# Three rotating tiles for transposed probabilities, later low halves and a later comparison step in a fused attention and expert kernel

## The chip, the core and the metric

The kernel runs on one core of a Trainium2 chip. The metric is the device time of one execution in microseconds, taken as the median of several runs; lower is better. The engines are named as the profile names them: PE is TensorE (PEld its weight loads), DVE is VectorE, ACT is ScalarE, POOL is GpSimd, SP is SyncE, which here only issues DMAs.

## What is computed

Attention over 4 batches, 8 heads, 576 positions and 64 dimensions, with a mask that keeps only scores near the row's maximum; then a feed-forward layer with a rational activation, then a second layer of experts. Cut to what matters:

```python
scores = scale * np.matmul(q, k.transpose(0, 1, 3, 2))
thresh = np.max(scores, axis=-1, keepdims=True) - tau
scores = np.where(scores >= thresh, scores, -1000000000.0)
attn = np.exp(scores - np.max(scores, axis=-1, keepdims=True))
attn = attn / (np.sum(attn, axis=-1, keepdims=True) + 1e-09)
x = np.matmul(attn, v)                      # then tokens x 512
h = x @ w_in                                # w_in, w_out arrive as float64
g = (a[0] + a[1]*h + a[2]*h**2 + a[3]*h**3) / (1.0 + abs(b[0])*abs(h) + abs(b[1])*h**2 + 1e-6)
x = g @ w_out                               # then top-1 routing over 8 experts
y[mask] = gate_w[mask, None] * (np.maximum(xc[mask] @ w1[e], 0.0) @ w2[e])
```

## The kernel before

**Precision.** Products that need more than one pass are made from a rounded high half and a low half (the value less its rounding). For K and Q, `high` (L256, L257) scales and rounds on ACT, and `low` (L268) subtracts on POOL. The weights `w_in` and `w_out` arrive as pairs of 32-bit words; `decode` turns them into single precision on DVE, POOL and ACT and then into two halves. It is a generator: each call runs on to the next `yield`, and `PACE_A` says how many calls lie between its steps. The steps are: load, shift (L115), merge (L117), `lf` on POOL (L121) with the exponent mask on DVE (L124), a product (L126), Abs on ACT (L129) and a sum on POOL (L130), the comparison and product on DVE (L133; on POOL, L135 and L136, for every fourth chunk), rounding on POOL (L142) and the low half (L146). The tile `w`, written by L129 and last read by L146, has one buffer, as have `t1` and `lf`.

**Tiling of attention.** Two heads make a pair, 16 pairs in all. Each pair has nine half tiles of queries (slots (r, h), r from 0 to 4), and the loop takes two slots a turn, so that a pair lasts 4.5 turns and there are 72 turns. In a turn, by the string `SEQ`, stand for the slots: the row minimum of the (negated) scores (M, L284), the threshold (H, L296), the exponential (E, L292), the products with V (V, L356 and L360), two evacuations of transposed tiles from the turn before (X, Y, L334), the output copy xT (W, L371), two entries of the task list (K, K), decoding (D, twice a turn), the mask with its sum (A, L302), the scores of the next turn's slots (N, L278), and the transposes of this turn's (t, L314). Each engine runs its own part of this string in order and waits on semaphores for the others. The order is thus written by hand.

**Buffers.** Scores have two PSUM buffers, so the scores of a slot of the next turn wait for the mask of this turn's. `P` holds the masked exponentials of an r (both h); four buffers, and two of `PL` for r = 4. The transposes of one pair go to `PT(p,0)` (r = 0, 1; 256 columns) and `PT(p,1)` (r = 2, 3, 4; 320 columns), one buffer each. At the end of a group one more tile T_x collects the last columns: for (p,1) it reads P(p,2) and P(p,3) (L321) and `PL` (L323, L324). The product with V of a group is ten steps (eight L356 matmuls in four pairs, two L360 with the remainder VZ), accumulated in the single PSUM buffer O. Its steps are handed out by a credit: each turn adds `CR`, up to `CAP` = 1.4, each step takes 0.48 or 0.59, and the turns with a T_x pay a surcharge. xT goes to DRAM (L375, L376) once a pair, after the second group.

**Tasks.** When a pair's first slot comes up, the loads of the pair after next are issued and eight tasks are listed for the next pair: high and low of two pieces of K and two of Q in turn. Two are taken each turn.

After turn 70 the pools of the stage close and the feed-forward units follow (`ffn1`, `actA` and on), then the experts.

Of the kernel before, what the change touches and what calls it, by code (L numbers as in the profile page):

```python
# [9 lines left out]
F32 = mybir.dt.float32  # L10
# [25 lines left out]
RG = (6, 8, 8)  # L36
C897 = 1.125 * 2.0 ** -15
DB = {"raw": 2, "t1": 1, "lf": 1, "w": 1}
PACE_A = (8, 1, 1, 1, 1, 2, 2, 2, 3)
PACE_B = (2, 1, 1, 1, 0, 1, 1, 0, 4)  # L40
CR = 1.4


@with_exitstack
def body(ctx, tc, q, k, v, tau, w_in, w_out, a, b, w_skip, w_gate, w1, w2, out):
# [6 lines left out]
    P = 128  # L52
# [147 lines left out]
    with ExitStack() as actx:  # L200
# [86 lines left out]
        def expo(p, r, h):  # L287
            st, m = St[p, r, h]
            if h == 0:
                Pt[p, r] = ap2.tile([P, 1152 if r < 4 else 576], F32, tag="P" if r < 4 else "PL", bufs=4 if r < 4 else 2, name=f"P{p}_{r}")  # L290
            e = Pt[p, r][:, 576 * h:576 * h + 576].rearrange("p (c x) -> p c x", c=2)
            nc.scalar.activation(e, st, AF.Exp, bias=m[:, 0:1], scale=-1.0)  # L292
            St[p, r, h] += [e]
# [12 lines left out]
        def transp(p, r, h):  # L306
            pt = Pt[p, r]
            g = 0 if r < 2 else 1
            if (p, g) not in PT:
                PT[p, g] = ap1.tile([P, 10, 256 if g == 0 else 320], F32, tag=f"PT{g}", name=f"PT{p}_{g}")  # L310
            T = psT.tile([P, 512], F32, tag="T", name=f"T{p}_{r}_{h}")
            for j in range(4):
                j0 = 128 * (5 * h + j)
                nc.tensor.transpose(T[:, 128 * j:128 * j + 128], pt[:, j0:j0 + 128], idn)  # L314
            Tt[p, r, h] = T
            if (r, h) not in ((1, 1), (4, 0)):
                return
            credit[0] -= 0.25 if r < 4 else 0.45
            T = Tt[p, r, 2] = psT.tile([P, 512], F32, tag="T", name=f"T{p}_{r}_x")
            for j in range(2):  # L320
                nc.tensor.transpose(T[:, 128 * j:128 * j + 128], Pt[p, 2 * g + j][:, 512:640], idn)  # L321
            if r == 4:
                nc.tensor.transpose(T[:, 256:384], Pt[p, 4][:, 448:576], swp)  # L323
                nc.tensor.transpose(T[0:64, 256:384], Pt[p, 4][:, 512:576], idn)  # L324
# [39 lines left out]
        def xout(p, g):  # L364
            bi, hp = divmod(p, NHP)
            o = Ot[g]
            w = 256 if g == 0 else 320
            if g == 0:
                xTs[p] = ap2.tile([P, 576], F32, tag="xT", name=f"xT{p}")
            xT = xTs[p]  # L370
            nc.scalar.activation(xT[:, 256 * g:256 * g + w], o[:, :w], AF.Copy)  # L371
            if g == 0:
                return
            c0, cl = xcols(bi)
            dq.append(lambda: [nc.sync.dma_start(xTd[:, hp, c0:c0 + 512], xT[:, 0:512]),  # L375
                               nc.sync.dma_start(xTd[:, hp, cl:cl + 64], xT[:, 512:576])])  # L376
            if hp == NHP - 1:
                wact.append(norm(bi))

        def norm(bi):  # L380
# [83 lines left out]
        for i in range(NS // 2 + 2):  # L464
# [4 lines left out]
            for x in cur:  # L469
                if x[1:] == (0, 0):  # L470
                    load(x[0] + 2)
                    n = x[0] + 1
                    for z in ((0, 0, 432), (0, 432, NK), (1, 0, 608), (1, 608, NQ)):
                        tasks += [(high, n, *z), (low, n, *z)]
                elif x[1:] == (2, 0):
                    loadv(x[0] + 1)
            mm = ap2.tile([P, 4], F32, tag="m", bufs=4, name=f"m{i}")
# [2 lines left out]
            for op in SEQ.split():  # L480
# [18 lines left out]
                elif c == "N" and j < len(nxt):  # L499
                    smm(*nxt[j])  # L500
                elif c == "M" and j < len(cur):
                    soft(*cur[j], mm[:, j:4:2])
                elif c == "H" and cur:
                    thr(mm)
                elif c == "E" and j < len(cur):
                    expo(*cur[j])
                elif c == "A" and j < len(cur):
                    mask(*cur[j])
                elif c == "T" and j < len(old):
                    transp(*old[j])  # L510
                elif c == "X" and j < len(old):
                    evac(*old[j])
                elif c == "Y" and j < len(old):
                    evac(*old[j])
                elif c == "t" and j < len(cur):
                    transp(*cur[j])
                elif c == "x" and j < len(cur):
                    evac(*cur[j])
                elif c == "V":
                    while pvq and credit[0] > 0 and not (xq and pvq[0][2] == 0):  # L520
                        credit[0] -= 0.48 if pvq[0][1] == 0 else 0.59
                        pv(*pvq.pop(0))
                elif c == "W":
                    while xq:
                        xout(*xq.pop())
                elif c == "K" and tasks:
                    fn, *n = tasks.pop(0)
                    fn(*n)
                elif c == "D" and i < 70:
                    wstep()  # L530
                elif c == "L":
                    for fn in late:
                        fn()
# [508 lines left out]
```

## Time and profile before

| what | us |
|---|---|
| median of 3 runs | 1034.93 (1033.43 to 1038.8) |
| the profiled execution | 1033.06 |
| its span, first to last instruction | 1031.2 |
| busy in the span: PE, DVE, ACT, POOL | 927.3, 698.6, 618.1, 480.2 |
| stage of attention (first row minimum to the last turn) | 13.6 to 363 |

The profile is of one execution. A row of the list of waits tells which engine and line stood idle, until what had ended, for how long in total, how often, and the longest. A row of the timeline tells the start, the duration, the engine, the line, the operation, what it writes and reads, and in brackets how long the engine had been idle and what ended that. Names are the program's, without buffer numbers.

### The profile page before, as it was taken

The numbers are of one execution on the slowest core, as the hardware profiler recorded it, in microseconds if no ns is written. First come the engines' busy times: TensorE is split into PE (matmuls) and PEld (weight loads), VectorE is DVE, ScalarE is ACT, GpSimd is POOL, SyncE is SP. The second block draws the span as 40 slices with busy tenths as digits, with TensorE's granted clock in tenths as the row PEclk, the third lists the DMA queues.
The fourth block names the chain that finished last, engine by engine and source line by source line (L and its number), as shares of the span: only waits on it lengthen the run. The fifth ranks groups of instructions, "written<-read, shape, count | busy, mean of one in ns | idle before, by whom it ended". The sixth has DMA issues, their size and how long they took to land.

```text
span 1031.2 us, 15811 instructions
## 1 busy us (share of the span) xinstructions
PE 927.3 (90%) x5442; PEld 760.5 (74%) x5442; DVE 698.6 (68%) x1450; ACT 618.1 (60%) x1153; POOL 480.2 (47%) x484
## 2 busy tenths in 40 slices
PE   3888888778768989999999999999998999999996
PEld 2556555555545668877888889889887888899885
DVE  4978877776776849989899987787776633211221
ACT  4777866767567757877777777777777611111110
POOL 1556548557557515678997663323334800000000
PEclk9989999888889999999999999999999999999998
DMA  5435345445262520434344232433424761313101
GB/s 152 110 103 154 88 135 137 137 119 162 92 185 63 186 79 23 147 103 147 113 170 156 75 123 103 140 127 106 171 92 158 251 215 62 123 61 123 62 31 33
DMA packets 72101, 124.14 MB, mean 120 GB/s; under 512 B 14928, under 2 KB 47184, under 8 KB 72016
## 3 DMA queue, kind: packets, MB, share of 16 engines
q1 hardware_dynamic: 67696, 99.48, 31.1%
q0 software_dynamic: 4320, 23.59, 6.6%
q8 instruction: 45, 0.74, 0.3%
q14 instruction: 40, 0.33, 0.1%
HBM read 85.22 MB, written 37.82 MB: 119 GB/s over the span
## 4 chain that ended last, share of the span: by engine, by line
PE 57%; POOL 11%; DVE 11%; issue 7%; ACT 7%; DMA 3%; SPq 2%; POOLq 0%; DVEq 0%; ACTq 0%
PE h L190 12%; PE acc L605 12%; PE mhs L190 10%; PE Ys L605 10%; PE S L278 4%; PE T L314 3%; PE O L356 3%; POOL Q L268 2%; POOL lf L126 1%; DVE m L284 1%; DVE p L634 1%; ACT P L292 1%; DVE h L649 1%; DVE p L646 1%; DVE h L647 1%
## 5 line engine op out<-in xcount | busy, mean ns | idle before, releaser
L605 PE MATMUL acc<-wo,g 128*128 128x512 f32 x864 | 223.4, 401 | 11.2 <-ACT g L655 8.2
L605 PEld LDWEIGHTS acc<-wo,g 128*128 128x128 f32 x864 | 158.7, 189 | 52.5 <-ACT g L655 13.0
L624 POOL TENSOR_TENSOR qd<-v,qd 128x384 f32<-128x384 f32 x96 | 98.5, 1026 | 188.0 <-ACT v L621 175.5
L278 PE MATMUL S<-K,Q 64*128 64x288 f32 x960 | 101.9, 337 | 78.4 <-DVE P L302 65.7
L190 PE MATMUL h<-xg,wi 128*128 128x384 f32 x864 | 165.2, 340 | 0.0
L278 PEld LDWEIGHTS S<-K,Q 64*128 64x128 f32 x960 | 76.9, 203 | 119.0 <-issue 83.0
L190 PEld LDWEIGHTS h<-xg,wi 128*128 128x128 f32 x864 | 152.1, 188 | 4.8 <-issue 0.4
L292 ACT ACTIVATE P<-S,m 128x576 f32<-128x576 f32 x144 | 101.0, 739 | 59.8 <-DVE m L284 59.3
L302 DVE SCALAR_TENSOR_TENSOR P<-S,m,P 128x576 f32<-128x576 f32 x144 | 111.5, 811 | 31.4 <-ACT P L292 31.3
L851 DVE SCALAR_TENSOR_TENSOR mgs<-mhs,mgs 128x384 fp32r<-128x384 f32 x48 | 26.8, 558 | 152.0 <-ACT mgs L850 152.0
L850 ACT ACTIVATE mgs<-mhs 128x384 fp32r<-128x384 f32 x48 | 23.6, 492 | 171.9 <-PE Ys L605 168.7
L284 DVE TENSOR_REDUCE m<-S 128x1 f32<-128x576 f32 x144 | 104.4, 753 | 28.6 <-PE S L278 26.6
L190 PE MATMUL mhs<-mxs,wss 128*128 128x384 f32 x576 | 109.2, 338 | 0.0
L605 PE MATMUL Ys<-wss,mgs 128*128 128x512 f32 x432 | 108.4, 396 | 0.0
L190 PEld LDWEIGHTS mhs<-mxs,wss 128*128 128x128 f32 x576 | 101.7, 188 | 4.0
L314 PE MATMUL T<-idn,P 128*128 128x128 f32 x576 | 93.7, 308 | 2.4 <-DVE P L302 2.3
L605 PEld LDWEIGHTS Ys<-wss,mgs 128*128 128x128 f32 x432 | 80.1, 188 | 16.1
L334 ACT ACTIVATE PT<-T 128x512 f32<-128x512 f32 x128 | 71.2, 600 | 28.4 <-PE O L360 28.2
L314 PEld LDWEIGHTS T<-idn,P 128*128 128x128 f32 x576 | 72.2, 157 | 16.3 <-issue 11.0
L629 DVE TENSOR_TENSOR p<-p,h 128x384 f32<-128x384 f32 x96 | 52.7, 549 | 43.9 <-ACT p L623 43.7
L356 PE MATMUL O<-PT,V 128*64 128x320 f32 (+1 forms) x512 | 79.6, 435 | 0.0
L268 POOL TENSOR_TENSOR K<-rk,K 128x432 fp32r<-128x432 f32 x30 | 33.8, 1125 | 94.1 <-ACT K L257 85.4
(149 smaller groups left out, 1547.5 us busy)
## 6 DMA issues: line engine op xcount, KB each, us to landing
xg<-xSd POOLq DMA_DIRECT2D x18, 768.0 KB, 5.7
x2Td<-x2h SPq DMA_DIRECT2D x12, 768.0 KB
mxs<-x2Td POOLq DMA_DIRECT2D x12, 768.0 KB, 5.6
rq<-in_q_dram SPq DMA_DIRECT2D x30, 304.0 KB, 4.3
raw<-in_moe_w_in_dram SPq DMA_DIRECT2D x16, 512.0 KB, 4.5
raw<-in_moe_w_out_dram SPq DMA_DIRECT2D x16, 512.0 KB, 3.9
rk<-in_k_dram SPq DMA_DIRECT2D x80, 72.0 KB, 3.0
xSd<-px SPq DMA_DIRECT2D x24, 192.0 KB, 1.9
```

The costliest lines, as they stand in the source:

```text
L190: nc.tensor.matmul(h, w[:, sw, 128 * k:128 * k + 128], x[:, sx, k], start=(k == 0 and i == 0), stop=(k == NKT - 1 and i == 2))
L268: eng.tensor_tensor(t[:, 1], x, t[:, 0].bitcast(F32), op=ALU.subtract)
L278: nc.tensor.matmul(st[:, c, :288], Q[d, x, q0:q0 + P], K[d, y, k0:k0 + 288], start=(s == 0 and j in (0, h)), stop=(s == 2 and (r < 4 or j ...
L284: nc.vector.tensor_reduce(m[:, 0:1], st, axis=AX.XY, op=ALU.min)
L292: nc.scalar.activation(e, st, AF.Exp, bias=m[:, 0:1], scale=-1.0)
L302: nc.vector.scalar_tensor_tensor(e, st, m[:, 1:2], e, op0=ALU.is_le, op1=ALU.mult, accum_out=sums[:, bi, col, hp:hp + 1])
L314: nc.tensor.transpose(T[:, 128 * j:128 * j + 128], pt[:, j0:j0 + 128], idn)
L334: nc.scalar.activation(dst[:, 5 * h:5 * h + 4, c0:c0 + 128], T.rearrange("p (j c) -> p j c", c=128), AF.Copy)
L356: nc.tensor.matmul(o[d, :w], vts[p][:, x, j, :], pt[:, j + 5 * x, :], start=(j == 0), stop=False)
L605: nc.tensor.matmul(ac[t], g[:, sg, 128 * t:128 * t + 128], w[:, sw, :], start=(first and i == 0), stop=(last and i == 2))
L624: nc.gpsimd.tensor_tensor(qd, v, u, op=ALU.mult)
L629: nc.vector.tensor_tensor(p, p, hs[c, f], op=ALU.mult)
```

## The change

PT becomes one tag with three buffers of the larger size for both groups. P goes from four buffers to three and PL from two to one. xT is split in two tiles of one buffer each, one for each group, and each is stored as soon as its group is done: three DMAs a pair where there were two. `CR` goes from 1.4 to 1.45. The task list is written in eight entries in which a low half stands one turn behind its high half, except the last; the rounding tasks keep their turns. In `PACE_A` the comparison step L133 (or L135 and L136) comes one call later, the rounding L142 too, and the low half L146 at the same call as before.

```diff
--- before.py
+++ after.py
@@ -36,9 +36,9 @@
 RG = (6, 8, 8)
 C897 = 1.125 * 2.0 ** -15
 DB = {"raw": 2, "t1": 1, "lf": 1, "w": 1}
-PACE_A = (8, 1, 1, 1, 1, 2, 2, 2, 3)
+PACE_A = (8, 1, 1, 1, 1, 3, 2, 1, 3)
 PACE_B = (2, 1, 1, 1, 0, 1, 1, 0, 4)
-CR = 1.4
+CR = 1.45
 
 
 @with_exitstack
@@ -287,7 +287,7 @@
         def expo(p, r, h):
             st, m = St[p, r, h]
             if h == 0:
-                Pt[p, r] = ap2.tile([P, 1152 if r < 4 else 576], F32, tag="P" if r < 4 else "PL", bufs=4 if r < 4 else 2, name=f"P{p}_{r}")
+                Pt[p, r] = ap2.tile([P, 1152 if r < 4 else 576], F32, tag="P" if r < 4 else "PL", bufs=3 if r < 4 else 1, name=f"P{p}_{r}")
             e = Pt[p, r][:, 576 * h:576 * h + 576].rearrange("p (c x) -> p c x", c=2)
             nc.scalar.activation(e, st, AF.Exp, bias=m[:, 0:1], scale=-1.0)
             St[p, r, h] += [e]
@@ -307,7 +307,7 @@
             pt = Pt[p, r]
             g = 0 if r < 2 else 1
             if (p, g) not in PT:
-                PT[p, g] = ap1.tile([P, 10, 256 if g == 0 else 320], F32, tag=f"PT{g}", name=f"PT{p}_{g}")
+                PT[p, g] = ap1.tile([P, 10, 320], F32, tag="PT", bufs=3, name=f"PT{p}_{g}")[:, :, :256 if g == 0 else 320]
             T = psT.tile([P, 512], F32, tag="T", name=f"T{p}_{r}_{h}")
             for j in range(4):
                 j0 = 128 * (5 * h + j)
@@ -365,16 +365,14 @@
             bi, hp = divmod(p, NHP)
             o = Ot[g]
             w = 256 if g == 0 else 320
-            if g == 0:
-                xTs[p] = ap2.tile([P, 576], F32, tag="xT", name=f"xT{p}")
-            xT = xTs[p]
-            nc.scalar.activation(xT[:, 256 * g:256 * g + w], o[:, :w], AF.Copy)
-            if g == 0:
-                return
+            xT = ap1.tile([P, w], F32, tag=f"xT{g}", name=f"xT{p}_{g}")
+            nc.scalar.activation(xT, o[:, :w], AF.Copy)
             c0, cl = xcols(bi)
-            dq.append(lambda: [nc.sync.dma_start(xTd[:, hp, c0:c0 + 512], xT[:, 0:512]),
-                               nc.sync.dma_start(xTd[:, hp, cl:cl + 64], xT[:, 512:576])])
-            if hp == NHP - 1:
+            c0 += 256 * g
+            dq.append(lambda: nc.sync.dma_start(xTd[:, hp, c0:c0 + 256], xT[:, 0:256]))
+            if g:
+                dq.append(lambda: nc.sync.dma_start(xTd[:, hp, cl:cl + 64], xT[:, 256:320]))
+            if g and hp == NHP - 1:
                 wact.append(norm(bi))
 
         def norm(bi):
@@ -470,8 +468,9 @@
                 if x[1:] == (0, 0):
                     load(x[0] + 2)
                     n = x[0] + 1
-                    for z in ((0, 0, 432), (0, 432, NK), (1, 0, 608), (1, 608, NQ)):
-                        tasks += [(high, n, *z), (low, n, *z)]
+                    z = ((0, 0, 432), (0, 432, NK), (1, 0, 608), (1, 608, NQ))
+                    tasks += [[(high, n, *z[0])], [], [(high, n, *z[1])], [(low, n, *z[0])], [(high, n, *z[2])],
+                              [(low, n, *z[1])], [(high, n, *z[3])], [(low, n, *z[2]), (low, n, *z[3])]]
                 elif x[1:] == (2, 0):
                     loadv(x[0] + 1)
             mm = ap2.tile([P, 4], F32, tag="m", bufs=4, name=f"m{i}")
@@ -524,8 +523,8 @@
                     while xq:
                         xout(*xq.pop())
                 elif c == "K" and tasks:
-                    fn, *n = tasks.pop(0)
-                    fn(*n)
+                    for fn, *n in tasks.pop(0):
+                        fn(*n)
                 elif c == "D" and i < 70:
                     wstep()
                 elif c == "L":
```

In the new file the output copy is L369 and its stores L372 and L374; lines behind these are one lower. How the order moves, at three places (the numbers behind the names are those of buffers; the first number of a name is the pair or the chunk):

On POOL, the low halves of pair 3 and the decoding beside them, before:

```order
L268 TENSOR_TENSOR K3_705<-rk3_400,K3_705 128x432
L142 TENSOR_SCALAR wo0_87<-w1_624 128x512
L268 TENSOR_TENSOR K3_705<-rk3_400,K3_705 128x432
L121 TENSOR_SCALAR lf2_760<-raw2_482 128x512
L146 TENSOR_TENSOR wo0_87<-w1_624,wo0_87 128x512
L126 TENSOR_TENSOR lf2_760<-lf2_760,t12_709 128x512
L268 TENSOR_TENSOR Q3_813<-rq3_401,Q3_813 128x608
L130 TENSOR_TENSOR lf2_760<-lf2_760,raw2_482 128x512
L268 TENSOR_TENSOR Q3_813<-rq3_401,Q3_813 128x608
```

and the same place with the change:

```order
L268 TENSOR_TENSOR K3_706<-rk3_400,K3_706 128x432
L142 TENSOR_SCALAR wo0_87<-w1_626 128x512
L121 TENSOR_SCALAR lf2_762<-raw2_482 128x512
L146 TENSOR_TENSOR wo0_87<-w1_626,wo0_87 128x512
L126 TENSOR_TENSOR lf2_762<-lf2_762,t12_710 128x512
L268 TENSOR_TENSOR K3_706<-rk3_400,K3_706 128x432
L130 TENSOR_TENSOR lf2_762<-lf2_762,raw2_482 128x512
L268 TENSOR_TENSOR Q3_815<-rq3_401,Q3_815 128x608 x2
```

The second low half of K and both of Q stand later, and the steps of wo0 and lf2 come ahead of them.

On DVE, around the comparison step of chunk 5, which is the row of line 133; before:

```order
L302 SCALAR_TENSOR_TENSOR P5_0_1427,sums_123<-S5_0_1_1447,m23_1478,P5_0_1427 128x576
L302 SCALAR_TENSOR_TENSOR P5_1_1488,sums_123<-S5_1_0_1455,m23_1478,P5_1_1488 128x576
L133 SCALAR_TENSOR_TENSOR w5_1479<-w5_1479,lf5_1416 128x512
L284 TENSOR_REDUCE m24_1532<-S5_1_1_1503 128x1
L284 TENSOR_REDUCE m24_1532<-S5_2_0_1511 128x1
L296 TENSOR_SCALAR m24_1532<-m24_1532,ptau_96 128x1 x2
L115 TENSOR_SCALAR t16_1557<-raw6_1318 128x512
L302 SCALAR_TENSOR_TENSOR P5_1_1488,sums_123<-S5_1_1_1503,m24_1532,P5_1_1488 128x576
```

and now:

```order
L302 SCALAR_TENSOR_TENSOR P5_0_1435,sums_123<-S5_0_1_1454,m23_1485,P5_0_1435 128x576
L302 SCALAR_TENSOR_TENSOR P5_1_1495,sums_123<-S5_1_0_1462,m23_1485,P5_1_1495 128x576
L284 TENSOR_REDUCE m24_1539<-S5_1_1_1510 128x1
L284 TENSOR_REDUCE m24_1539<-S5_2_0_1518 128x1
L296 TENSOR_SCALAR m24_1539<-m24_1539,ptau_96 128x1 x2
L133 SCALAR_TENSOR_TENSOR w5_1486<-w5_1486,lf5_1424 128x512
L115 TENSOR_SCALAR t16_1565<-raw6_1326 128x512
L302 SCALAR_TENSOR_TENSOR P5_1_1495,sums_123<-S5_1_1_1510,m24_1539,P5_1_1495 128x576
```

The step has gone from ahead of the two row minima to behind the thresholds, ahead of the masks.

On PE, the products with V of pairs 4 and 5 (O4_1, then O5_0) between the scores S and the transposes T; before:

```order
L356 MATMUL O4_1_1545<-PT4_1_1336,V4_1017 64x320 x2
L278 MATMUL S5_3_1_1617<-K5_1210,Q5_1315 128x288 x6
L278 MATMUL S5_4_0_1625<-K5_1210,Q5_1315 128x288 x12
L314 MATMUL T5_2_1_1638<-idn_63,P5_2_1543 128x128 x4
L314 MATMUL T5_3_0_1643<-idn_63,P5_3_1604 128x128 x4
L360 MATMUL O4_1_1545<-PT4_1_1336,VZ1_125 64x320 x2
L278 MATMUL S6_0_0_1667<-K6_1438,Q6_1554 128x288 x6
L278 MATMUL S6_0_1_1675<-K6_1438,Q6_1554 128x288 x6
```

and now:

```order
L356 MATMUL O4_1_1552<-PT4_1_1344,V4_1020 64x320 x2
L360 MATMUL O4_1_1552<-PT4_1_1344,VZ1_125 64x320 x2
L278 MATMUL S5_3_1_1630<-K5_1220,Q5_1322 128x288 x6
L278 MATMUL S5_4_0_1638<-K5_1220,Q5_1322 128x288 x12
L314 MATMUL T5_2_1_1651<-idn_63,P5_2_1550 128x128 x4
L314 MATMUL T5_3_0_1656<-idn_63,P5_3_1611 128x128 x4
L356 MATMUL O5_0_1673<-PT5_0_1479,V5_1303 64x256 x6
L278 MATMUL S6_0_0_1686<-K6_1446,Q6_1561 128x288 x6
L278 MATMUL S6_0_1_1694<-K6_1446,Q6_1561 128x288 x6
```

The two closing products of O4_1 have gone one turn up, and O5_0 begins one turn earlier.

## Rows read from the trace of the kernel before

**Rows 1.** The page's first two parts: busy time by engine, granted clock by slice.

```profile
PE 927.3 (90%) x5442; PEld 760.5 (74%) x5442; DVE 698.6 (68%) x1450; ACT 618.1 (60%) x1153; POOL 480.2 (47%) x484
...
PEclk9989999888889999999999999999999999999998
```

**Rows 2.** Table by stretches: stretch, length, busy PE, PEld, DVE, ACT, POOL, granted clock, DMA.

```profile
13.60:363.00 349.40, 282.42 (x2209) 197.62 (x2209) 272.48 (x645) 245.35 (x448) 205.86 (x197) 0.91 0.46 132
139.50:142.90 3.40, 3.40 (x18) 2.85 (x17) 1.56 (x4) 2.28 (x5) 3.32 (x3) 0.50 0.92 217
363.00:1031.00 668.00, 642.74 (x3224) 561.44 (x3223) 422.54 (x797) 368.37 (x698) 273.11 (x278) 0.99 0.34 115
```

**Rows 3.** List of waits, 13.6 to 363 us: total us, times, longest.

```profile
POOL K L268 <- ACT K L257: 85.4, 25, 19.1
...
PE S L278 <- DVE P L302: 65.7, 38, 7.0
...
POOL Q L268 <- ACT Q L257: 44.1, 17, 7.9
DVE P L302 <- ACT P L292: 29.3, 15, 4.0
DVE m L284 <- PE S L278: 26.6, 41, 2.6
ACT PT L334 <- PE O L360: 24.9, 15, 4.8
DVE w L133 <- POOL lf L130: 15.4, 8, 3.9
ACT w L129 <- POOL wo L146: 12.2, 5, 4.3
...
PE S L278 <- POOL Q L268: 1.0, 1, 1.0
```

**Rows 4.** Timeline at 134.9 us: start, us, engine, line, operation, out<-in, wait.

```profile
134.94 0.76 PE L360 MATMUL O<-PT,VZ 128*64 128x320 f32 x4
135.77 0.60 ACT L334 ACTIVATE PT<-T 128x512 f32<-128x512 f32 x1 [3.80 <-PE O L360]
...
136.87 1.36 ACT L292 ACTIVATE P<-S,m 128x576 f32<-128x576 f32 x2
```

**Rows 5.** Timeline of DVE: masks behind a PT wait, first and last of six.

```profile
137.63 0.82 DVE L302 SCALAR_TENSOR_TENSOR P<-S,m,P 128x576 f32<-128x576 f32 x1 [2.60 <-ACT P L292]
...
365.09 0.82 DVE L302 SCALAR_TENSOR_TENSOR P<-S,m,P 128x576 f32<-128x576 f32 x1 [2.04 <-ACT P L292]
```

**Rows 6.** Timeline at 71 us, POOL and DVE: a comparison step behind lf.

```profile
70.94 1.27 POOL L130 TENSOR_TENSOR lf<-lf,raw 128x512 f32<-128x512 f32 x1
...
72.25 0.69 DVE L133 SCALAR_TENSOR_TENSOR w<-w,lf 128x512 f32<-128x512 f32 x1 [1.74 <-POOL lf L130]
```

**Rows 7.** Single lines, 133 and 268: durations in ns, least, median, most.

```profile
L133 DVE SCALAR_TENSOR_TENSOR w<-w,lf x12: 685/838/1933, 37.4 to 300.1; 128x512 f32<-128x512 f32 x12
...
L268 POOL TENSOR_TENSOR Q<-rq,Q x30: 1469/1482/1922, 27.7 to 347.7; 128x608 fp32r<-128x608 f32 x30
```

**Rows 8.** Timeline: masks behind a wait for wo, first and last of three.

```profile
104.44 0.82 DVE L302 SCALAR_TENSOR_TENSOR P<-S,m,P 128x576 f32<-128x576 f32 x1 [3.06 <-ACT P L292]
...
251.04 1.48 POOL L268 TENSOR_TENSOR Q<-rq,Q 128x608 fp32r<-128x608 f32 x1
...
252.47 1.26 POOL L146 TENSOR_TENSOR wo<-w,wo 128x512 fp32r<-128x512 f32 x1
...
253.76 0.66 ACT L129 ACTIVATE w<-raw 128x512 f32<-128x512 f32 x1 [4.31 <-POOL wo L146]
...
255.09 0.82 DVE L302 SCALAR_TENSOR_TENSOR P<-S,m,P 128x576 f32<-128x576 f32 x1 [3.95 <-ACT P L292]
```

**Rows 9.** Timeline at 258.5 us: exponentials of pair 11 and T_x of pair 10.

```profile
258.53 1.41 ACT L292 ACTIVATE P<-S,m 128x576 f32<-128x576 f32 x2 [0.73 <-DVE m L284]
258.72 0.63 PE L321 MATMUL T_x<-idn,P 128*128 128x128 f32 x2
```

**Rows 10.** Single line 375, the stores of xT issued by SP: durations in ns.

```profile
L375 SPq DMA_DIRECT2D xTd<-xT x16: 319/530/1328, 51.2 to 378.3; - x16
```

## Prediction

> **What bounds the kernel now.** The page comes first: TensorE is busy 90% of the span, yet the line of granted clock dips in the first third and hardly after [rows 1]. The table by stretches then parts the span. From 13.6 to 363 us, the 72 turns of the attention stage, no engine is full: TensorE 282 of 349 us, VectorE 272, ScalarE 245, GpSimd 206, at a mean granted clock of 0.91; from 363 us on the clock is 0.99 [rows 2]. So the first stage is bound by waits in a ring (reduce, exponential, mask, next scores), and the rest by TensorE. All that is changed lies in the first stage; what follows should slide with it.
>
> A mean turn is 349.4 / 72 = 4.85 us, of which VectorE works 272.5 / 72 = 3.78. Its idle time has three large causes in the list of waits [rows 3]: ScalarE's exponential (29.3 us in 15 waits), the scores from TensorE (26.6 in 41) and the decoder's lf from GpSimd (15.4 in 8). ScalarE's own list says why its exponential is late: it stood before evacuations into PT until the product O had ended (24.9, 15 waits), and before the decoder's Abs until GpSimd had finished a low half wo (12.2, 5 waits) [rows 3]. GpSimd in turn stood 85.4 + 44.1 us before low halves of K and Q until ScalarE had rounded them [rows 3].
>
> **Part A, three PT tiles and CR.** Now PT1 has one buffer: the first evacuation of a pair's second group waits for the last product of the pair before. One case in full: O ends at 134.94 + 0.76, PT starts at 135.77, the exponential queued behind it at 136.87, VectorE's mask at 137.63 after 2.60 us idle [rows 4, 5]. Six such cases stand at pairs 5, 7, 9, 11, 13 and 15, of 2.04 to 3.30 us on VectorE, 15.9 in sum (the first and the last are shown) [rows 5]. With three buffers PT(p,1) takes what PT(p-1,0) had, whose products are over a turn or more before. Besides, CR 1.45 puts the two closing products of O4_1 a turn earlier, so that even one buffer would be free in time. Either way the wait goes; what is next late is VectorE itself, since the scores are reduced by then. A = 15.9; bounds 0 (the wait moves to another product) and 15.9.
>
> **Part B, the comparison step.** VectorE waits for lf up to 3.9 us in eight of twelve steps L133 [rows 3]; the shown one starts 0.04 us after lf's end at 72.21 and keeps the masks behind it back [rows 6]. The step now stands one call, half a turn, later: 4.85 / 2 = 2.4 us. That covers all but about 1.5 us of the longest (3.9). lf itself comes no later, since a low half of K whose rounding is a turn old stands before it in place of a fresh one of Q. Against that, eight of the twelve steps move from behind the masks, where they share time with the wait for scores, to ahead of them, and four the other way: 4 more times 0.69 us (the shortest L133) on the ring [rows 7], of which I count 2. B = 15.4 - 1.5 - 2 = 12; bounds 0 (POOL late by the same half turn) and 15.4.
>
> **Part C, low halves a turn behind.** ScalarE's Abs waits for wo's low half, the last reader of the one w tile. Three of the five waits reach VectorE: 3.06, 3.06 and 3.95 us, 10.1 in sum [rows 8]. In the last one GpSimd runs Q low at 251.04, wo low at 252.47, and ScalarE starts at 253.76 after 4.31 idle. The new order drops the low half of K ahead of wo1 in the first case (0 left). In the second K8's takes the place of Q8's and the backlog ahead starts earlier (1 left). In the third wo's low half still follows a Q low half that needs the rounding of the same turn, 1.48 + 1.26 of 4.31 [rows 7, 8], so 2.4 of 3.95 are left. C = 3.06 + 2.06 + 1.5 = 6.6; bounds 0 and 10.1.
>
> **Part D, the clock.** A mean of 0.91 with levels of 1.2 and 2.4 GHz means 18% of the stage, 63 us, at the lower one. A stretch at the lower level lies right behind a long wait: TensorE is full at 139.5 to 142.9 with a clock of 0.50 [rows 2], right behind one of the pauses in which its scores wait for a mask (65.7 us in 38) [rows 3]. Fewer such pauses mean fewer such stretches; they can show only in VectorE's 26.6 us of waiting for scores. I take 4, bounds 0 and 13 (half).
>
> **Costs.** P has three buffers in place of four: the exponential of P(p+1,1) now waits for the first T_x transpose of pair p, which reads P(p,2). At pair 10, at the lower clock, T_x starts at 258.72 and its two take 0.63; the second exponential of the pair shown starts at 258.53 + 0.7 [rows 9]. So the margin is about 0.2 us even there: 0.5 in all, at most 0.63 in each of eight even pairs, 5. Behind it on ScalarE stand the PT evacuations, and VectorE's second mask waits for it. The Q low halves, now both in the fourth turn, gate the next pair's scores; TensorE waited 1.0 us once for one [rows 3]. I take 1.5, at most 1.48 for each of eight odd pairs, 12. The sixteen extra stores of xT cost SyncE some 0.53 us each [rows 10], hidden because loads are issued two pairs ahead; xT's single buffers have a pair (4.5 turns) to drain. If that cover went it would be 8. The high half's later step on GpSimd waits for nothing new: none.
>
> L133 takes 0.69 to 1.93 us, median 0.84; I add 1 for the new neighbours [rows 7]. The Trainium skill ("SBUF — State Buffer", Who interferes with whom) says that a VectorE instruction with two SBUF inputs and a GpSimd instruction that reads SBUF shut each other out for the whole of whichever began first; the mask, with one input in PSUM, would be spared. That speaks against a step moved beside two Q low halves in a row; the spread in the row agrees with it. By the rule met at every step the sum would be that of the last rival below; by the row's median it is the 1 us just taken. Costs: 0.5 + 1.5 + 1 = 3.
>
> **Giving back.** A + B + C = 34.5 us of VectorE idling go, but TensorE uses part of it to catch up: 282 us of work would have to fit into some 315. I let a quarter, 8.6 us, come back as waiting for scores, the row of 26.6 us [rows 3] growing instead of shrinking in places. Sum: 15.9 + 12 + 6.6 + 4 - 3 - 8.6 = 26.9 us. The profiled execution took 1033.06 us (span 1031.2), so 1006; the median of the three runs, 1034.93, is 1.9 higher, so the forecast for a median is **1008 us**, its own range 999 to 1016.
>
> **The rivals** (times as medians).
> *TensorE takes the place.* In the turns with 13 transposes and 12 products it is the late one: A shrinks to 6, B to 6, C to 3, D to 0, costs 3: 12 us, **1023**. For it: the scores are already waited for most often (41 waits). Against: these waits are short (mean 0.65).
> *More than forecast.* Nothing comes back and the clock pays more: 34.5 + 6 - 3 = 37.5, **997**. For it: turns without a decoding step and without those waits run at VectorE's 3.8 us.
> *No change.* The ring of three P tiles ties ScalarE to TensorE by 0.63 x 8 = 5 us, the SyncE cover goes (8), and half of A moves to the product O itself, which has one PSUM buffer: 34.5 x 0.5 - 5 - 8 = 4, **1031**. Nor would it count that the ring does nothing because CR alone clears the wait; that alters no time.
> *Slower.* GpSimd falls behind, so that the two Q low halves end after the scores need them in every pair: 15 x 2 x 1.48 = 44 us lost against 26.9 gained, **1052**. It decides from 26.9 / 15 = 1.8 us of lateness a pair. For it: GpSimd worked without a pause around 250 us, and TensorE stood behind it. Against: its 129.5 us of waiting for ScalarE [rows 3] are what the later slot removes, and it is busy 59% of the stage [rows 2].
> *The moved steps collide.* Each of twelve L133 takes the longest time shown, 12 x (1.93 - 0.84) = 13 us [rows 7]: 26.9 + 1 - 13 = 15, **1020**. For it: the longest one; against: half of them are at 0.84 or less with GpSimd busy 59% of the time. The section of the Trainium skill named above is the rule behind it.
>
> **Chances.** Forecast 0.47, TensorE 0.19, more 0.18, collision 0.05, no change 0.07, slower 0.04. Leaving out a tenth at each side: from 991 (the high case with its clock term at 12) to 1027 (the TensorE case with P's 5). Some 0.5%, 5.2 us, is what a measurement tells from no change; so faster 0.88 (the forecast, more, collision and nearly all of the TensorE case), same 0.08, slower 0.04.
>
> **What would show it.** In the list of waits of after: no ScalarE PT wait on O above 0.5 us (A), VectorE w on lf under 3 us in sum (B), ScalarE w on wo 3 to 6 (C), a clock of 0.93 or more in the stage (D), GpSimd's waits on ScalarE for K and Q below 60 us. Scores waiting for GpSimd's Q above 5 us, or the exponential for T_x above 3, would be the costs mis-sized. The forecast is wrong if the stage's end, now at 363, stays above 350, or if what follows takes other than its 668 us by over 3.

## The result and the profile after

The changed kernel takes **983.27 us** (median, 982.5 to 985.22) against 1034.32 us: a ratio of 0.950, 95% interval 0.947 to 0.953, or 51 us less. The forecast was 1008 us, a gain of 27, with a range of 991 to 1027. The direction was right; the size was not, and the time lies outside the range.

The profiled execution spans 983.4 us against 1031.2, 47.8 us less. The missing 3.2 us are the choice of executions: the profiled one of before was 1.3 us under its median, that of after (985.22) 1.9 us over its own. All sums below are made on the spans.

The page of after, its busy line and its granted clock by slice (answers to [rows 1]):

```profile
PE 913.0 (93%) x5442; PEld 749.5 (76%) x5442; DVE 701.1 (71%) x1450; ACT 618.1 (63%) x1153; POOL 483.3 (49%) x484
...
PEclk9999999999999999999999999999998999999998
```

The table by stretches, same columns as [rows 2]; the attention stage now ends at 316.7 us, not 363:

```profile
13.60:316.70 303.10, 266.67 (x2211) 184.17 (x2211) 275.35 (x644) 246.20 (x452) 208.05 (x188) 0.98 0.54 152
316.70:983.20 666.50, 644.16 (x3221) 563.81 (x3219) 422.36 (x798) 367.48 (x695) 274.05 (x287) 0.99 0.34 115
```

The list of waits of that stage (answers to [rows 3]: total us, times, longest):

```profile
POOL Q L268 <- ACT Q L257: 44.4, 22, 5.0
POOL K L268 <- ACT K L257: 38.8, 15, 19.1
PE S L278 <- DVE P L302: 36.5, 35, 5.2
DVE m L284 <- PE S L278: 15.0, 38, 0.8
...
DVE P L302 <- ACT P L292: 9.8, 11, 2.8
...
ACT w L129 <- POOL wo L146: 4.6, 3, 2.8
...
ACT P L292 <- PE T_x L321: 0.9, 2, 0.4
```

Where the 47.8 us went: the stage is 46.3 us shorter, the rest 1.5. That rest is a matter of where the stage is cut: the last of the six waits that part A counted (2.04 us, ahead of the mask at 365.09 [rows 5]) lies behind 363. From the end of the last mask on, both kernels take the same, 664.5 us before and 665.0 after. In the stage VectorE's busy time rose by 2.9 (272.48 to 275.35), so its idle time fell by 49.2, from 76.9 to 27.8. Three rows make up most of it: waiting for the exponential 29.3 to 9.8 (19.5), for lf 15.4 to no row at all (15.4), and for scores 26.6 to 15.0 (**11.6**). ScalarE's row of PT behind O is gone too. The first two sum to 34.9, where the prediction had 34.5 for A, B and C; the third was forecast to grow. The clock of the stage rose from 0.91 to 0.98, and TensorE's busy time fell by 15.8 us (282.42 to 266.67) for the same products.

VectorE is now busy 275 of 303 us in the stage. Its longest wait left is the one that C did not clear: Q low, then wo low on GpSimd, ScalarE's w behind it, VectorE's mask, and TensorE's scores. Timeline of POOL, ACT, DVE and PE (start, us):

```profile
222.96 1.48 POOL L268 TENSOR_TENSOR Q<-rq,Q 128x608 fp32r<-128x608 f32 x1 [2.01 <-ACT Q L257]
224.40 1.27 POOL L146 TENSOR_TENSOR wo<-w,wo 128x512 fp32r<-128x512 f32 x1
...
225.70 0.67 ACT L129 ACTIVATE w<-raw 128x512 f32<-128x512 f32 x1 [2.81 <-POOL wo L146]
...
227.03 0.82 DVE L302 SCALAR_TENSOR_TENSOR P<-S,m,P 128x576 f32<-128x576 f32 x1 [2.85 <-ACT P L292]
...
228.00 1.28 PE L278 MATMUL S<-K,Q 64*128 64x288 f32 x10 [2.66 <-DVE P L302]
```

and the table by stretches of the pause and of what lies behind it (the clock is the last but two):

```profile
223.80:228.00 4.20, 1.54 (x14) 0.80 (x13) 1.35 (x6) 2.30 (x5) 4.12 (x4) 1.00 0.56 140
228.00:232.50 4.50, 4.43 (x26) 3.56 (x28) 4.29 (x10) 4.02 (x9) 4.24 (x5) 0.62 0.73 200
```

Behind the pause TensorE is full for 4.5 us at a mean clock of 0.62. This is the pattern of [rows 2]. Read in stretches of 2 us, the granted clock falls below 0.7 at four places of the stage (near 39, 186, 230 and 254 us), where before had fifteen.

### The profile page after: what moved, and what is told of

It reads as the page before. It is cut to its first block, busy times and chain, and to the rows that moved or that the text cites. A ratio compares the mean times of both kernels' runs of the same rounds, so it can differ in the third digit from the quotient of the medians.

```text
span 983.4 us, 15831 instructions
## 1 busy us (share of the span) xinstructions
PE 913.0 (93%) x5442; PEld 749.5 (76%) x5442; DVE 701.1 (71%) x1450; ACT 618.1 (63%) x1153; POOL 483.3 (49%) x484
## 4 chain that ended last, share of the span: by engine, by line
PE 62%; DVE 15%; ACT 6%; POOL 6%; issue 5%; DMA 3%; SPq 3%; POOLq 0%; DVEq 0%; ACTq 0%
PE acc L604 14%; PE h L190 14%; PE mhs L190 10%; PE Ys L604 10%; PE S L278 4%; DVE m L284 3%; PE O L356 3%; PE T L314 3%; DVE P L302 2%; DMA rq<-in_q_dram 1%; ACT P L292 1%; SPq L225 1%; POOL Q L268 1%; DVE p L633 1%; DVE t L115 1%
## 5 line engine op out<-in xcount | busy, mean ns | idle before, releaser
L278 PE MATMUL S<-K,Q 64*128 64x288 f32 x960 | 97.2, 323 | 47.9 <-DVE P L302 36.5
L278 PEld LDWEIGHTS S<-K,Q 64*128 64x128 f32 x960 | 72.1, 191 | 88.9 <-issue 50.2
L850 DVE SCALAR_TENSOR_TENSOR mgs<-mhs,mgs 128x384 fp32r<-128x384 f32 x48 | 26.8, 558 | 151.1 <-ACT mgs L849 151.1
L314 PE MATMUL T<-idn,P 128*128 128x128 f32 x576 | 86.2, 291 | 0.0
L314 PEld LDWEIGHTS T<-idn,P 128*128 128x128 f32 x576 | 66.0, 147 | 12.6 <-issue 10.9
L616 ACT ACTIVATE qd<-h 128x384 f32<-128x384 f32 x96 | 46.6, 485 | 45.4 <-PE h L190 45.2
```

The lines of the kernel that those rows point to most:

```text
L278: nc.tensor.matmul(st[:, c, :288], Q[d, x, q0:q0 + P], K[d, y, k0:k0 + 288], start=(s == 0 and j in (0, h)), stop=(s == 2 and (r < 4 or j ...
L616: nc.scalar.activation(u, h, AF.Abs)
```

## The experiments

All times are medians. The ratio is to the kernel before, run beside it on the same chip.

| kernel | what differs | us | ratio, interval |
|---|---|---|---|
| after | | 983.27 | 0.950, 0.947–0.953 |
| u_ring | after, one PT buffer a group | 985.96 | 0.953, 0.950–0.956 |
| u_cr | after, CR 1.4 | 986.22 | 0.952, 0.949–0.955 |
| u_ring_cr | both of these | 1005.14 | 0.971, 0.969–0.973 |
| u_low | after, low halves as before | 1004.37 | 0.970, 0.967–0.973 |
| u_pace | after, old pace of decoding | 985.76 | 0.953, 0.951–0.955 |
| d_ring | before, with the buffers only | 1010.0 | 0.975, 0.973–0.977 |
| d_low | before, with the later low halves only | 1012.11 | 0.976, 0.974–0.979 |
| d_pace | before, with the new pace only | 1025.18 | 0.990, 0.988–0.992 |
| a_pause | after, 15 pauses put in | 1029.7 | 0.995, 0.994–0.997 |
| a_pause_fill | the same, 16 products in each | 1035.14 | 1.001, 0.999–1.003 |
| a_fill | after, the 16 products alone | 1034.19 | 0.999, 0.998–1.001 |
| a_pf7 | a_pause, 7 products in each | 1025.6 | 0.991, 0.987–0.994 |
| a_f7 | after, the 7 products alone | 1002.75 | 0.968, 0.965–0.971 |
| v_best | after, room of PT spent otherwise | 982.01 | 0.950, 0.947–0.952 |

### Which part bought what

One part undone at a time, in the changed kernel:

```
u_ring     -  PT[p, g] = ap1.tile([P, 10, 320], F32, tag="PT", bufs=3, ...)
           +  PT[p, g] = ap1.tile([P, 10, 256 if g == 0 else 320], F32, tag=f"PT{g}", ...)
u_cr       -  CR = 1.45
           +  CR = 1.4
u_ring_cr  both of these
u_low      -  tasks += [[(high, n, *z[0])], [], [(high, n, *z[1])], [(low, n, *z[0])], ...]
           +  tasks += [[(f, n, *x)] for x in z for f in (high, low)]
u_pace     -  PACE_A = (8, 1, 1, 1, 1, 3, 2, 1, 3)
           +  PACE_A = (8, 1, 1, 1, 1, 2, 2, 2, 3)
```

> The kernel after, with one PT buffer for each group as before; CR 1.45 and all else stay. If the third buffer is what clears ScalarE's wait for the product O, the PT waits on O come back (24 us in 15 on ScalarE) and the time goes to 983 + 16 to 25 = 999 to 1008. If the closing products that CR moves a turn up do it alone, the time stays at 983 (within 3) and the list of waits shows PT waiting for O for under 3 us.

> The kernel after, with CR back at 1.4, three PT buffers kept. If the ring clears the PT wait by itself: 983 to 986, no PT wait on O over 1 us. If CR does it: 999 or more, as the closing products again stand a turn later. If both are needed for TensorE's even load, some 988 with the scores waited for longer than 15 us.

> The kernel after, with one PT buffer a group and CR 1.4 together; later low halves and comparison step kept. Either alone cleared ScalarE's wait for O (0.8 us or less). Without both it must be back in the odd pairs, 20 to 25 us on ScalarE. If part A was rightly sized at 15.9 of VectorE: 984 + 16 = 1000. If each wait costs more than itself, because TensorE is at the lower clock behind it: 1005 or more and a mean clock of 0.96 or less in the stage. If the freed slots absorb it: under 992.

> The kernel after, with the low halves back beside their roundings. The theory that GpSimd's waits for ScalarE made lf and wo late: GpSimd waits 129 us for K and Q again in place of 83, ScalarE waits for wo 10 us or more in place of 4.6, and the time goes up by 6 (part C as forecast) to 12. The rival, that the half turn given to the comparison step is enough for the whole: within 3 us of 983.

> The kernel after, with the decoder's pace as before. If the later comparison step is what clears VectorE's wait for lf: this wait is back at 8 to 15 us and the time is 993 to 1003. If the low halves a turn later made lf early enough on their own: the wait stays under 4 us and the time within 4 of 983.

**Buffers and CR** do the same thing: either alone costs at most some 3 us against having both, which their intervals don't tell from nothing; both undone cost 22. The waits of u_ring_cr's stage show PT behind O back, and with it the two rows of VectorE:

```profile
DVE P L302 <- ACT P L292: 23.8, 15, 3.5
DVE m L284 <- PE S L278: 23.0, 38, 2.2
ACT PT L334 <- PE O L360: 22.6, 16, 3.4
```

The exponential is waited for 14.0 us more than in after, the scores 8.0 more. So in the changed kernel part A is worth its wait and over half as much again in a row that it does not touch.

**Low halves** are worth 21 us when undone. The waits of u_low's stage:

```profile
DVE m L284 <- PE S L278: 21.6, 44, 1.8
DVE P L302 <- ACT P L292: 17.2, 13, 3.7
ACT w L129 <- POOL wo L146: 12.5, 6, 3.7
DVE w L133 <- POOL lf L130: 3.9, 3, 1.8
```

Three rows of VectorE rise against after: the exponential by 7.4 (C was put at 6.6), the scores by 6.6, and lf by 3.9, though the new pace is in place. The 21 us are more than the 6 to 12 expected, and GpSimd's waits for ScalarE's K and Q came to 95.9 us, not 129. **The pace** alone, undone, costs 2.5 us, within the intervals: with the low halves late, lf is waited for 4.5 us even at the old pace:

```profile
DVE w L133 <- POOL lf L130: 4.5, 3, 1.7
```

One part done at a time, in the kernel before, is the other half of this:

```
d_ring     the PT, P, PL and xT lines of the change (CR stays 1.4)
d_low      the new list of tasks and its loop (CR, PACE_A, buffers stay)
d_pace     -  PACE_A = (8, 1, 1, 1, 1, 2, 2, 2, 3)
           +  PACE_A = (8, 1, 1, 1, 1, 3, 2, 1, 3)
```

> The kernel before, with the three PT buffers (P three, PL one, xT in two) alone; CR 1.4, low halves and pace as before. PT's wait for O falls from 25 to under 2 us. By the prediction's A: 1034 - 16 = 1018. If the wait only uncovers GpSimd's lateness (wo, lf) or scores: 1026 or more, with those two waits longer than 27.6 together.

> The kernel before, with the later low halves alone. If the low halves are the larger half of the gain, as undoing them suggests (20 us): 1014 or less, ScalarE's wait for wo at 5 us or less, VectorE's for lf at 5 or less, PT's wait for O as before (25). By the prediction's C alone: 1027.

> The kernel before, with the new pace alone. By the prediction's B: VectorE's wait for lf falls from 15.4 to 3 or less and the time by 10 to 12, 1022. If the later step only moves the wait, since GpSimd is late for another reason: over 1029, with the wait for wo still at 12.

Alone they gain 25.9, 24.4 and 10.3 us by their ratios (of 1034.3), 60.6 in sum, where together they gain 51. Buffers took 8 us less than the 1018 expected, low halves came in below their 1014, and the pace fell between its two figures. The runs with one part undone give the pairs: low halves and pace (u_ring_cr) gain 30.2 us of 34.7, buffers with CR and pace (u_low) 31.5 of 36.2, buffers with CR and low halves (u_pace) 48.9 of 50.3. Each ratio is good to some 2 us, so this suggests, and no more, that the overlap goes with the pace. For its pair with the low halves the reason is on record: in d_low, with the old pace, lf is down from 15.4 to 4.9 us, and in d_pace, by the step alone, to 2.9. The line of d_low:

```profile
DVE w L133 <- POOL lf L130: 4.9, 3, 1.8
```

So B's wait was cured twice: by the step that goes later, and by GpSimd, which no longer stands in front of fresh roundings when lf is due. The prediction gave all of it to the step. What the pace shares with the buffers was not traced.

The waits for scores go the other way: alone no part does much for them. The rows of d_ring, d_low and d_pace, in this order:

```profile
DVE m L284 <- PE S L278: 23.8, 38, 2.7
...
DVE m L284 <- PE S L278: 24.8, 37, 3.1
...
DVE m L284 <- PE S L278: 27.1, 43, 3.1
```

Against 26.6 before that is 2.8 and 1.8 us less and 0.5 more, at stage clocks of 0.92, 0.95 and 0.93; all parts together brought 11.6 less at 0.98. That fits the clocks: the pauses that a single part leaves still have slow stretches behind them.

### Why the waits for scores fell

Two explanations stood. A pause may be dearer than its length, since TensorE works at the lower clock behind it and the scores of the next turns come late. Or the scores were late by TensorE's amount of work, and fell for some reason of order. The test makes pauses in the changed kernel that have nothing to do with its buffers or low halves: eight idle copies on ScalarE ahead of every fourth turn's exponentials, fifteen in all. Then TensorE is given products with a zero matrix zz to fill them, which leave O as it is (PAUSE is turns 8 to 64 in steps of 4, NFILL 16 or 7; a_pause has the first piece, a_fill and a_f7 the others, a_pause_fill and a_pf7 all):

```
 elif c == "E" and j < len(cur):
+    if j == 0 and i in PAUSE:
+        for _ in range(8):
+            nc.scalar.activation(dmy, dmy, AF.Copy)
     expo(*cur[j])
...
 elif c == "V":
+    todo = i in PAUSE
     while pvq and credit[0] > 0 and not (xq and pvq[0][2] == 0):
         credit[0] -= 0.48 if pvq[0][1] == 0 else 0.59
+        if todo and pvq[0][2] > 0:
+            fill(*pvq[0][:2])
+            todo = False
         pv(*pvq.pop(0))
...
+def fill(p, g):
+    w = 256 if g == 0 else 320
+    for n in range(NFILL):
+        d = slice(64 * (n % 2), 64 * (n % 2) + 64)
+        nc.tensor.matmul(Ot[g][d, :w], zz, PT[p, g][:, n % 4, :], start=False, stop=False)
```

> The changed kernel with eight idle ScalarE copies (128x288, about 0.36 us each by the 0.44 us of a 128x320 evacuation, 2.9 us together) ahead of the first exponential of every fourth turn from 8 to 64, fifteen turns. ScalarE's slack ahead of the exponential is 45.9 us in 42 waits, about 0.6 a turn, so the pauses alone cost 15 x 2.3 = 34 us. Theory that a pause costs more than itself (TensorE works at the lower clock behind it and then brings the scores late): VectorE's waits for scores grow from 15.0 to 24 or more, the stage's clock falls from 0.98 to below 0.94, and the kernel takes 983 + 34 + 10 = 1027 us or more. Rival that TensorE catches up during a pause (the step of giving back in the prediction): waits for scores stay at 15 or fall, and the kernel takes 1005 to 1018 us whatever the clock.

The copies took 3.75 us a turn, not 2.9 (0.44 us each). The table by stretches and the waits of a_pause's stage:

```profile
13.60:362.00 348.40, 283.88 (x2211) 198.03 (x2211) 271.73 (x645) 297.05 (x573) 206.89 (x197) 0.91 0.47 133
```

```profile
PE S L281 <- DVE P L305: 65.2, 38, 5.9
...
DVE P L305 <- ACT P L295: 46.7, 24, 4.1
DVE m L287 <- PE S L281: 25.3, 40, 2.5
```

Fifteen pauses add 36.9 us of waiting for the exponential, and 10.3 us of waiting for scores come with them. The clock is back at 0.91, TensorE's busy time at 284 us, and the scores' row at 25 us: within about 1.5 us, the figures of the kernel before. The rival, that TensorE catches up in a pause, is out for these pauses.

> The same eight idle ScalarE copies in the same fifteen turns, and in each of these turns sixteen TensorE products with a zero matrix that add nothing to O, issued between the products ahead of the scores that stand in the pause: some 2 to 2.5 us of work (0.13 to 0.16 us each) in a pause of about 3.4. Theory of the clock: the pauses no longer bring the lower level, so the stage's clock is 0.96 or more, waits for scores fall back below 18, and the kernel is 6 to 12 us faster than with the pause alone, though TensorE does some 35 us more work. Rival (scores late by TensorE's amount of work): the kernel is as slow as with the pause alone or slower by up to 15 us.

> The sixteen zero products in the same fifteen turns without the pause, as a control of their own price. TensorE works 263 / 72 = 3.65 us of a turn of 4.2, so 2.2 more make these turns 1 to 1.7 us longer: both theories expect 983 + 15 to 25 = 998 to 1008 us, with waits for scores up by that much. If it costs nothing the products don't stand where they were meant to and the run with pause and products tells nothing.

The sixteen products were too many: 63.3 us of TensorE, 4.2 a turn and not the 2 to 2.5 expected, where the pauses had 2 to 4. The clock came back to 0.98, but the waits for scores stayed at 27.1 us and the kernel took 5.4 us more than with the pauses alone, which by the words of the expectation is the rival's outcome. Alone the products cost 51 us, where 15 to 25 were expected, so their own length can be the reason, and the pair of runs separates nothing. The next pair has seven.

> The pause and the zero products of the run before, but seven products a turn in place of sixteen: sixteen took 63.3 / 15 = 4.2 us of TensorE a turn and so more than filled the pause of 3.1 to 4.1 us; seven take 1.85. With the pause alone the kernel took 1029.7 us, with a clock of 0.91 in the stage and 25.3 us of waits for scores. Theory of the clock: these products keep it at 0.96 or above, and since they fit in the pause the waits for scores fall back to 15 to 19 us, 1029.7 - 8 = 1019 to 1024 us. Rival (the scores behind a pause are late for another reason than the clock, or TensorE's amount of work decides): clock up or not, waits for scores stay at 23 or more and the kernel at 1028 to 1035.

> Seven zero products in the same fifteen turns without the pause, the control for their own price: 1.85 us more of TensorE in turns of 4.2 with 3.65 of work, so 15 x 1.3 = 20 us at most and 983 + 10 to 20 us by both theories, with waits for scores of 25 to 35 us. So if the same products make the kernel with the pauses faster, it is not because they are free.

Table by stretches and waits of a_pf7's stage:

```profile
13.60:356.00 342.40, 294.76 (x2421) 200.61 (x2421) 276.96 (x644) 295.65 (x572) 207.65 (x197) 0.98 0.47 135
```

```profile
DVE P L308 <- ACT P L298: 46.4, 22, 4.1
DVE m L290 <- PE S L284: 15.0, 32, 1.4
```

and the one row of a_f7's stage that matters:

```profile
DVE m L288 <- PE S L282: 32.9, 43, 3.0
```

The pauses of ScalarE are all there (46.4 us), TensorE is busy 11 us more (in a_f7 the same products add 24, 290.85 against 266.67, so its other work took some 13 less), and yet the waits for scores are back at the 15.0 us of after, with the clock. Without pauses the same products cost 19.5 us and raise that row to 32.9; so they help only where they stand in a pause. One turn of each shows it. First a_pause, its timeline (TensorE's scores after the pause, VectorE's reduce of the next turn) and its table for the 4.5 us behind the pause:

```profile
177.94 1.81 PE L281 MATMUL S<-K,Q 64*128 64x288 f32 x12 [3.12 <-DVE P L305]
...
185.02 1.42 DVE L287 TENSOR_REDUCE m<-S 128x1 f32<-128x576 f32 x2 [2.52 <-PE S L281]
```

```profile
177.90:182.40 4.50, 4.46 (x24) 3.59 (x26) 4.16 (x10) 4.47 (x11) 2.62 (x3) 0.50 0.71 246
```

Then the same turn of a_pf7:

```profile
175.81 1.31 PE L284 MATMUL S<-K,Q 64*128 64x288 f32 x12 [1.40 <-DVE P L308]
...
180.54 1.44 DVE L290 TENSOR_REDUCE m<-S 128x1 f32<-128x576 f32 x2 [0.17 <-PE S L284]
...
184.29 0.76 DVE L290 TENSOR_REDUCE m<-S 128x1 f32<-128x576 f32 x1 [0.51 <-PE S L284]
```

```profile
175.80:180.30 4.50, 4.49 (x38) 2.93 (x38) 4.01 (x11) 4.47 (x11) 2.35 (x3) 1.00 0.82 280
```

At a clock of 0.50 (1.2 GHz) TensorE got 24 matmul records done in the 4.5 us behind the pause and the reduce waited 2.52 us; at 1.00 (2.4 GHz) it got 38 done, none of them zero products, and the same reduce waited 0.17, the one a turn later 0.51.

The kernel's time says the same with less room: 1025.6 against 1029.7 us, with intervals that overlap by a hair, a little over the 1019 to 1024 expected. The 10.3 us are not all kept because VectorE's busy time rose from 271.7 to 277.0 us, all of it in four decoding steps (44.2 to 49.9 us). That they met GpSimd's work at other points is likely by what stands below, but not shown.

### A version with the freed room

Since CR alone clears the wait, one PT buffer a group is enough, and its room goes to four P and two PL buffers and a second w.

```
-DB = {"raw": 2, "t1": 1, "lf": 1, "w": 1}
+DB = {"raw": 2, "t1": 1, "lf": 1, "w": 2}
...
-Pt[p, r] = ap2.tile([P, 1152 if r < 4 else 576], F32, ..., bufs=3 if r < 4 else 1, name=f"P{p}_{r}")
+Pt[p, r] = ap2.tile([P, 1152 if r < 4 else 576], F32, ..., bufs=4 if r < 4 else 2, name=f"P{p}_{r}")
...
-PT[p, g] = ap1.tile([P, 10, 320], F32, tag="PT", bufs=3, ...)
+PT[p, g] = ap1.tile([P, 10, 256 if g == 0 else 320], F32, tag=f"PT{g}", ...)
```

> The changed kernel with one buffer for each PT group again (CR 1.45 stays, the earlier run with one buffer took the same time), and with the room that this frees: four P and two PL buffers as before, and two buffers for the decoder's w. What is left to gain in the changed kernel by its list of waits: ScalarE's w on wo 4.6 us in 3, of which the 2.8 us one stands behind the longest pause of TensorE left, and the exponential on T_x 0.9. Theory that each removed wait gives itself and about half of it again at the clock: 983 - 5 = 978, down to 976. Rival that these waits lie beside the scores: no change, 983 to 986.

```profile
13.60:315.00 301.40, 262.38 (x2210) 180.99 (x2211) 276.65 (x644) 246.54 (x451) 207.91 (x197) 0.99 0.54 153
```

```profile
DVE m L284 <- PE S L278: 14.3, 34, 0.8
DVE P L302 <- ACT P L292: 5.7, 9, 1.6
```

The wait of w on wo is gone and the exponential is waited for 4.1 us less, but VectorE waits 1.0 for lf again and is busy 1.3 longer. The stage is 1.7 us shorter, and the kernel, at 982.01 us, can't be told from the changed one. The rival of no change was the better forecast: with VectorE busy 277 of 301 us little is left to take from waits.

## Why the prediction was wrong

The sum by its own terms, on the spans (us gained):

| term | predicted | measured |
|---|---|---|
| waits removed in A, B and C, gross | 15.9 + 13.9 + 6.6 = 36.4 | 19.5 + 15.4 = 34.9 |
| costs, the busy 2 us of B included | -5 | -2.9 |
| D and giving back: waits for scores | 4 - 8.6 = -4.6 | +11.6 |
| smaller idle times, and the rest | 0 | 2.7 + 1.5 |
| sum | 26.8 (26.9 there, B rounded up) | 47.8 |

The first two lines agree in net, 31.4 against 32.0. (With the 2.04 us of A's last wait, which stands in the rest, the removed waits are 36.9.) **The step that failed is "giving back"**, with the clock term D beside it: 16.2 of the 20.9 us missed. The prediction let TensorE take a quarter of the removed idle time back, since 282 us of work would have to fit into some 315. But the 282 us were no fixed amount: part of it was the same work at half speed, and when the pauses went it shrank to 266.67. The prediction saw the slow stretches, and wrote that fewer pauses mean fewer of them; then it priced them at 4 and set 8.6 against them by an argument that took their busy time for work. The runs put the row the other way round: fifteen pauses, 36.9 us in all, bring 10.3 us of waits for scores, and filling the pauses takes them away. In the change itself nothing separates the clock from the rest; there it is this test, and the same clock and busy time in a_pause as before the change, that speak for it.

Part by part:

- **A** was the right wait (no ScalarE row of PT on O is left) and its mechanism right to both halves: buffers or CR, either one does it. Its worth with both undone is 22 us, because of the scores' row; 15.9 was its own wait only. Put alone into the kernel before (d_ring) it clears 15.7 us of the exponential's row and 2.8 of the scores'.
- **B**: the wait went in full, 15.4 for 13.9. But the later step was not needed for it: d_low and u_pace show that late low halves nearly free lf by themselves, and d_pace that the step does so too. The size was right with half of the cause, which is in part luck. The prediction named the place, GpSimd's older K low half ahead of lf in place of a fresh one of Q, but drew from it only that lf comes no later.
- **C**: the wait for wo is 4.6 us, in the 3 to 6 named, and the case that was to remain does, at 2.85 us on VectorE for the 2.4 worked out. What C does to lf and to the scores was not in the term: alone (d_low) it takes 8.0 us from the exponential's row and 10.5 from that of lf.
- **Costs**: the exponential behind T_x costs 0.9 us in 2 waits, and no score waited for a Q low half. Neither limit named was passed. The 3 us for VectorE's steps were right in sum (2.9) and wrong in place: L133 did not get longer but shorter (below).
- **The test by GpSimd** failed: its waits for ScalarE's K and Q are 83.2 us, not under 60. They were 129.5; the one row of ScalarE behind GpSimd in the list is the 4.6 us of wo.
- **The rest** of the kernel took 1.5 us less, within the 3 named, and that for A's last wait: it slid as a block.

Of the rivals, "more than forecast" (997) had the direction of the error, but even there the clock was put at 6, and the range, which ended at its high case with a clock term of 12, stopped 8 us short. "TensorE takes the place", with the largest chance of the others, pointed the wrong way: its row, the waits for scores, shrank by 11.6 us where it was to grow.

## What to carry to other kernels

Where TensorE's granted clock drops behind each pause, count a removed pause at its own length plus what the slow stretch delays, which depends on how many pauses are left: pauses put back into the changed kernel brought 0.3 to 0.6 us of waiting for scores for each us of pause, while one kind taken out of the kernel before gave back 0.2 at most. And don't take TensorE's busy time in a stage of 0.91 for work that must fit. When several edits feed one engine's queue, price them in combination: here two edits cured the same wait, two others were alternatives, and only removing pairs or adding singles showed which. After the change ask which engine is full now: at 275 of 303 us VectorE leaves little for another wait to give.

## What the runs showed of the hardware

Two of VectorE's decoding steps, which take their inputs from SBUF, took longer in sum, and the long ones stand beside instructions of GpSimd. Groups by line in the stage of before (count, then busy us and mean ns):

```profile
L117 DVE SCALAR_TENSOR_TENSOR raw<-raw,t 128x512 uint32<-128x512 uint32 x16 | 13.5, 846 | 0.0
L133 DVE SCALAR_TENSOR_TENSOR w<-w,lf 128x512 f32<-128x512 f32 x12 | 12.7, 1060 | 15.5 <-POOL lf L130 15.4
...
L115 DVE TENSOR_SCALAR t<-raw 128x512 uint32<-128x512 uint32 x16 | 6.7, 420 | 0.0
```

and of after:

```profile
L117 DVE SCALAR_TENSOR_TENSOR raw<-raw,t 128x512 uint32<-128x512 uint32 x16 | 16.4, 1022 | 0.0
...
L115 DVE TENSOR_SCALAR t<-raw 128x512 uint32<-128x512 uint32 x16 | 10.7, 669 | 0.0
L133 DVE SCALAR_TENSOR_TENSOR w<-w,lf 128x512 f32<-128x512 f32 x12 | 10.6, 880 | 0.0
```

L115 and L117 together cost 6.9 us more; L133, for which the prediction feared it, cost 2.1 less (12.7 to 10.6). Of the sixteen L115 of after, the six beside no GpSimd instruction took 0.41 to 0.45 us; of the ten beside one, seven took 0.63 to 1.34. One place of after, POOL and DVE:

```profile
117.39 1.53 POOL L268 TENSOR_TENSOR K<-rk,K 128x432 fp32r<-128x432 f32 x1 [1.28 <-ACT K L257]
...
117.87 1.34 DVE L115 TENSOR_SCALAR t<-raw 128x512 uint32<-128x512 uint32 x1
...
120.23 1.49 POOL L268 TENSOR_TENSOR Q<-rq,Q 128x608 fp32r<-128x608 f32 x1 [1.31 <-ACT Q L257]
...
120.60 1.66 DVE L117 SCALAR_TENSOR_TENSOR raw<-raw,t 128x512 uint32<-128x512 uint32 x1
```

L115 began at 117.87 inside K's low half and ended 0.29 us after it (119.21 against 118.92); L117 began at 120.60 inside Q's and ended 0.54 us after it (122.26 against 121.72). The masks, with their scores in PSUM, took 0.82 us at most, though 103 of the 142 in the stage ran beside a GpSimd instruction. For L115 and L117 this agrees with the rule of the Trainium skill ("SBUF — State Buffer", Who interferes with whom) that whoever begins first holds the shared ports for its whole instruction, and it fits here for L115 too, a step with one SBUF input.

The Trainium skill ("TensorE: Matmul & The Clock Gate", HAM oscillation — how this bites in real kernels) prices a pause-ridden kernel by the time at the lower clock times one half. By the rows here that would be an estimate of 349.4 x 0.18 / 2 = 31 us before and 303.1 x 0.04 / 2 = 6 after, a fall of 25; the waits for scores, where the prediction looked for it, fell by 11.6. Here TensorE was not the full engine in the stage, so much of the slow time could lie beside VectorE's work; how it divides was not measured.
